# Attention of the next batch interleaved with the inverse transform and projection of this one, with the PSUM banks split 3 and 5

## The chip, the cores and the metric

The kernel runs on one core of one Trainium2 chip. The core has a matrix engine (PE, with its weight loads PEld), a vector engine (DVE), a scalar engine (ACT), a general engine (POOL, which also issues most loads) and a queue engine (SP, which issues the stores). Each engine takes its instructions strictly in the order in which they stand in its queue, and waits on semaphores for the others. The metric is the device time of one execution in microseconds (us). An execution is also profiled: the profile gives the span from the first to the last instruction.

## The reference

Shapes: 8 batches, 8 heads, 576 positions, 64 channels per head; `p` holds 32 packed queries per head. What is computed, cut to what matters:

```python
def sm_attn(qq, kk, vv):                       # softmax attention, scale 1/8
    a = softmax(scale * qq @ kk.T)
    return a @ vv
p_packed = sm_attn(p, k, v)                    # 32 rows per head
x = heads_to_columns(sm_attn(q, p_packed, p_packed))     # [8, 576, 512]
x1, x2, x3 = split(x @ w_proj, 3)              # each [8, 576, 512]
x2_conv = irfft(rfft(x2, axis=1) * rfft(filter, axis=0), n=576, axis=1)
out = (x1 * x2_conv * x3) @ w_out
```

## The kernel before

All loops over batches are unrolled by Python. A scheduler of the framework sets each engine's queue from the order in which the code is written, and may move an instruction ahead when its inputs are due. Tiles come from pools; when a pool has no free buffer, the next writer waits for the last reader of the one that it takes. PSUM has eight banks, and each PSUM tile here takes one.

The work of a batch `b` is written as six stages. `att1`: turn the keys (`kTp`, evicted to `kT` by DVE and ACT in turn), scores of the packed queries (`s1`), their exponentials (`e1`, ACT), the weighted values (`pv`) and sums (`z1`), normalisation (`ppn`, DVE), and the turn of the result (`ppT`) into a buffer `R` (`ppk` in the trace). `att2`: turn the queries (`qTp`, `qTtp`), second scores (`s2`), exponentials (`e2`), sums (`zs`, `zr`, DVE), normalised weights (`a2n`, POOL), and the projection of the packed rows (`qp`, evicted by ACT to `qm`). `att3`: forward transform of the weights (`fp`, `fpt`, evicted by ACT to `fa`) and their turn (`a2tp`, to `a2t`). `moe1`: the spectrum (`f0` to `f4`), its product with the filter's (four DVE products `tt0` to `tt3` from PSUM, two POOL sums, giving `gm`, which has five parts). `moe2`: for eight pieces (four column groups by two halves) two matmuls each for `x1` and `x3`, five for `x2` from `gm` (the inverse transform), an ACT copy `x1s`, and two DVE products `w` and `y`. `moe3`: five output tiles `o` from `y`, scaled by ACT into `os`, stored by SP.

In the loop, iteration `b` writes the attention of `b + 1` first and then the `moe` stages of `b`. All PSUM tiles share one ring of eight banks (`pst`). Before the loop stand the preparation of the filter (`prologue_filter`), the first part of `pack_p` (the packed queries of batch 0), `att1(0)`, the second part of `pack_p` (batches 1 to 7), `att2(0)` and `att3(0)`.

Of the kernel before, what the change touches and what calls it, by code (L numbers as in the profile page):

```python
# [16 lines left out]
P = 128  # L17
# [59 lines left out]
def kernel(  # L77
# [132 lines left out]
    def att1(b):  # L210
        kn, vn, qn, qt = loaded[b]
        e1 = sb.tile([KP, KI, HJ], FP16, tag="e1", name=f"e1_b{b}")
        for g in range(H // 2):
            tp = pst(f"kTp_b{b}", [P, 2, 3, KP], FP16)
            for hh in range(2):
                for ii in range(3):
                    nc.tensor.transpose(tp[:, hh, ii, :], kn[:, 2 * g + hh, ts(ii, P)], ident[0:KP, 0:KP])  # L217
            kT = sb.tile([P, 2, 3, KP], FP16, tag="kT", name=f"kT_b{b}", bufs=4)
            if g % 2 == 0:
                nc.vector.tensor_copy(out=kT[:], in_=tp[:])  # L220
            else:
                nc.scalar.copy(out=kT[:], in_=tp[:])  # L222
            s1 = pst(f"s1_b{b}", [KP, 2, KI, NPK])
            for hh in range(2):
                for ii in range(3):
                    nc.tensor.matmul(s1[:, hh, 2 * ii:2 * ii + 2, :], kT[:, hh, ii, :], pk[:, b, 2 * g + hh, :],  # L226
                                     start=True, stop=True)
            nc.scalar.activation(  # L228
                out=e1[:, :, g * 2 * NPK:(g + 1) * 2 * NPK].rearrange("p i (h j) -> p h i j", h=2),
                in_=s1[:], func=AF.Exp, scale=scale)  # L230
        pv = pst(f"pv_b{b}", [P, 2, 4 * D])
        z1 = pst(f"z1_b{b}", [P, 2])
        for t in range(2):
            for i in range(KI):
                nc.tensor.matmul(pv[:, t, :], e1[:, i, ts(t, P)], vn[:, 4 * t:4 * t + 4, ts(i, D)],  # L235
                                 start=(i == 0), stop=(i == KI - 1))
            for i in range(KI):
                nc.tensor.matmul(z1[:, t:t + 1], e1[:, i, ts(t, P)], ones[0:KP, :],
                                 start=(i == 0), stop=(i == KI - 1))
        rz1 = sb.tile([P, 2], FP32, tag="rz1", name=f"rz1_b{b}")  # L240
        nc.vector.reciprocal(rz1[:], z1[:])
        ppn = sb.tile([P, 2, D], FP16, tag="ppn", name=f"ppn_b{b}")
        for u in range(4):
            r = slice(32 * u, 32 * u + 32)
            nc.vector.tensor_tensor(out=ppn[r, :, :], in0=pv[r, :, ts(u, D)],  # L245
                                    in1=rz1[r, :].unsqueeze(2).broadcast_to([32, 2, D]), op=ALU.mult)
        pT = pst(f"ppT_b{b}", [P, 2, P], FP16)
        for t in range(2):
            for u in range(2):
                nc.tensor.transpose(pT[u * D:(u + 1) * D, t, :], ppn[:, t, :], ident[:])  # L250
        R = rings[b % NR]
# [3 lines left out]
        st[b] = dict(R=R)  # L255

    def att2(b):
        kn, vn, qn, qt = loaded.pop(b)
        s = st[b]
        R = s["R"]  # L260
        Rd = R.rearrange("p (g a) c -> p g (a c)", a=2)
        qT = sb.tile([P, H, 2, P], FP16, tag="qT", name=f"qT_b{b}")
        qTt = sb.tile([P, H // 2, 64], FP16, tag="qTt", name=f"qTt_b{b}")
        for c in range(2):
            tp = pst(f"qTp_b{b}", [P, 4, 2, P], FP16)
            for hh in range(4):
                for ii in range(2):
                    nc.tensor.transpose(tp[:, hh, ii, :], qn[:, 4 * c + hh, ts(ii, P)], ident[:])  # L268
            nc.vector.tensor_copy(out=qT[:, 4 * c:4 * c + 4, :, :], in_=tp[:])
        tp = pst(f"qTtp_b{b}", [P, H // 2, 64], FP16)  # L270
        for g in range(H // 2):
            nc.tensor.transpose(tp[:, g, :], qt[:, 2 * g:2 * g + 2, :], ident[0:64, 0:64])
        nc.vector.tensor_copy(out=qTt[:], in_=tp[:])
# [4 lines left out]
        for ii in range(3):  # L278
# [21 lines left out]
        s["a2n"] = a2n  # L300
        qm = sb.tile([P, 2, DM3], FP16, tag="qm", name=f"qm_b{b}")
        for c in (1, 0, 2):
            for t in range(2):
                qp = pst(f"qp_b{b}", [P, DM])
                for u in range(2):
                    g = 2 * t + u
                    nc.tensor.matmul(qp[u * D:(u + 1) * D, :], Rd[:, g, NPK:3 * NPK], wp[:, g, ts(c, DM)],
                                     start=True, stop=True)
                nc.scalar.copy(out=qm[:, t, ts(c, DM)], in_=qp[:])  # L309
        s["qm"] = qm  # L310

    def att3(b):
        s = st[b]
        a2n = s["a2n"]
        fa = sb.tile([P, 2, 640], FP16, tag="fa", name=f"fa_b{b}")
        for t in range(2):
            fp = pst(f"fp_b{b}", [P, DM])
            for i in range(5):
                n = TILE_SZ[i]
                nc.tensor.matmul(fp[:], a2n[0:n, i, ts(t, P)], wc[0:n, i, 0:DM], start=(i == 0), stop=(i == 4))  # L320
            nc.scalar.copy(out=fa[:, t, 0:DM], in_=fp[:])
        fp = pst(f"fpt_b{b}", [P, 2, 64])
# [7 lines left out]
        a2t = sb.tile([P, 2, S], FP16, tag="a2t", name=f"a2t_b{b}")  # L330
# [6 lines left out]
        s["fa"] = fa  # L337
        s["a2t"] = a2t

    def moe1(b):  # L340
        s = st[b]
        fa, qm = s["fa"], s["qm"]
        gm = sb.tile([P, 5, DM], FP16, tag="gm", name=f"gm_b{b}")
# [7 lines left out]
        for m in range(2):  # L351
            fre = spectrum(m)
            fim = spectrum(2 + m)
            tt = [sb.tile([P, DM], FP32, tag=f"tt{j}", name=f"tt{j}_b{b}", bufs=2) for j in range(4)]
            nc.vector.tensor_tensor(out=tt[0][:], in0=fre[:], in1=hre[:, m, :], op=ALU.mult)
            nc.vector.tensor_tensor(out=tt[1][:], in0=fim[:], in1=him[:, m, :], op=ALU.mult)  # L356
            nc.vector.tensor_tensor(out=tt[2][:], in0=fre[:], in1=him[:, m, :], op=ALU.mult)
            nc.vector.tensor_tensor(out=tt[3][:], in0=fim[:], in1=hre[:, m, :], op=ALU.mult)
            nc.gpsimd.tensor_tensor(out=gm[:, m, :], in0=tt[0][:], in1=tt[1][:], op=ALU.subtract)  # L359
            nc.gpsimd.tensor_tensor(out=gm[:, 2 + m, :], in0=tt[2][:], in1=tt[3][:], op=ALU.add)  # L360
        ft = spectrum(4)
        nc.vector.tensor_tensor(out=gm[:, 4, :], in0=ft[:], in1=htail[:], op=ALU.mult)
        s["gm"] = gm

    def moe2(b):
        s = st[b]
        a2t, qm, gm = s["a2t"], s["qm"], s["gm"]
        y = sb.tile([P, ND, S], FP16, tag="y", name=f"y_b{b}")
        for m in range(ND):
            for e in range(2):  # L370
                cols = ds(e * HALF, HALF)
                x1 = pst(f"x1_b{b}", [P, HALF])
                x3 = pst(f"x3_b{b}", [P, HALF])
                x2 = pst(f"x2_b{b}", [P, HALF])
                for t in range(2):
                    nc.tensor.matmul(x1[:], qm[:, t, ts(m, P)], a2t[:, t, cols], start=(t == 0), stop=(t == 1))  # L376
                for t in range(2):
                    nc.tensor.matmul(x3[:], qm[:, t, ds(2 * DM + m * P, P)], a2t[:, t, cols],  # L378
                                     start=(t == 0), stop=(t == 1))
                for j in range(5):  # L380
                    nc.tensor.matmul(x2[:], gm[:, j, ts(m, P)], ac[:, j, cols], start=(j == 0), stop=(j == 4))  # L381
                x1s = sb.tile([P, HALF], FP32, tag="x1s", name=f"x1s_b{b}", bufs=3)
                nc.scalar.copy(out=x1s[:], in_=x1[:])  # L383
                w = sb.tile([P, HALF], FP32, tag="w", name=f"w_b{b}", bufs=3)
                nc.vector.tensor_tensor(out=w[:], in0=x1s[:], in1=x3[:], op=ALU.mult)  # L385
                nc.vector.scalar_tensor_tensor(out=y[:, m, cols], in0=w[:], scalar=SC_Y, in1=x2[:],  # L386
                                               op0=ALU.mult, op1=ALU.mult)
        s["y"] = y

    def moe3(b):  # L390
        y = st.pop(b)["y"]
        for i in range(5):
            n = TILE_SZ[i]
            o = pst(f"o_b{b}", [P, DM])
            for m in range(ND):
                nc.tensor.matmul(o[0:n, :], y[:, m, COL0[i]:COL0[i] + n], wout[:, m, :], start=(m == 0), stop=(m == ND - 1))  # L396
# [4 lines left out]
            else:  # L401
                tl = out[b, 512:576, :].rearrange("(p e) c -> e p c", e=2)
                nc.sync.dma_start(tl[0], os_[0:32, :])
                nc.sync.dma_start(tl[1], os_[32:64, :])

    pack_p(0, 1, "a")
    prologue_filter()
    att1(0)
    pack_p(1, B, "b")
    att2(0)  # L410
    att3(0)
# [40 lines left out]
```

## Time and profile before

| | |
|---|---|
| median of 3 runs | 357.73 us (356.91 to 357.97) |
| the profiled execution | 357.62 us, its span 355.8 us |
| PE matmul busy, weight loads | 281.9 us (79%), 170.7 us (48%) |
| DVE, ACT, POOL busy | 161.6, 127.1, 94.7 us |
| granted TensorE clock, mean | 0.865 of full speed |
| data read, written | 35.80 MB, 9.44 MB |

Lines with "L" name a line of the kernel's source. Busy time of an engine is the union of its instructions; a matmul's recorded end includes its run-out through the array, so consecutive matmuls overlap in the record, and the distance from one start to the next tells what one costs. A row "x6" is a merged run of six instructions. In square brackets stands how long the engine was idle before a row, and what released it. In rows by stretch, "PEclk" is the share of full clock that the throttle granted.

### The profile page before, as it was taken

How to read it: one execution, taken by the hardware profiler on the slowest of the kernel's cores; microseconds unless marked ns; L12 is line 12 of the kernel's file. 1: busy time of each engine (PE TensorE's matmuls, PEld its weight loads, DVE VectorE, ACT ScalarE, POOL GpSimd, SP SyncE). 2: the span in 40 equal slices, each digit the busy share in tenths (PEclk: the TensorE clock that was granted, in tenths of full speed). 3: DMA queues.
4: the chain of work that ended last, by engine and by line, in shares of the span. 5: the costliest groups of instructions: out<-in, count | busy, mean ns of one | idle time of the engine just before them, and what ended most of it. 6: DMA issues, size and time to landing. Idle time of an engine off the chain costs nothing.

```text
span 355.8 us, 5499 instructions
## 1 busy us (share of the span) xinstructions
PE 281.9 (79%) x2162; PEld 170.7 (48%) x2162; DVE 161.6 (45%) x376; ACT 127.1 (36%) x259; POOL 94.7 (27%) x106
## 2 busy tenths in 40 slices
PE   0596777789868896789777896789778896889995
PEld 0135625536454464546354464546354455546462
DVE  2401721548233851648223851648233941648481
ACT  1324153242516234333516144333516144333333
POOL 7240320344015500433015500433002500133230
PEclk9997675699958998599959998699968997599999
DMA  7999961940369004920378014930300012000303
GB/s 274 216 194 203 201 89 9 144 49 3 133 84 118 0 33 116 157 29 2 133 91 110 1 50 109 143 33 3 133 2 0 0 62 72 2 1 3 134 2 133
DMA packets 35626, 29.08 MB, mean 82 GB/s; under 512 B 7888, under 2 KB 30416, under 8 KB 35600
## 3 DMA queue, kind: packets, MB, share of 16 engines
q0 software_dynamic: 29408, 16.52, 35.2%
q1 hardware_dynamic: 5904, 10.65, 8.7%
q10 hardware_dynamic: 288, 1.56, 1.1%
q8 instruction: 17, 0.28, 0.3%
q14 instruction: 9, 0.07, 0.1%
HBM read 35.80 MB, written 9.44 MB: 127 GB/s over the span
## 4 chain that ended last, share of the span: by engine, by line
PE 61%; DVE 14%; POOL 11%; ACT 6%; issue 3%; DMA 3%; POOLq 0%; DVEq 0%; ACTq 0%
PE x_b L381 11%; PE o_b L396 10%; PE pv_b L235 6%; POOL gm_b L359 6%; PE fp_b L320 5%; PE s_b L226 5%; PE hp L204 4%; PE qTp_b L268 4%; DVE zs_b L291 3%; DMA pnat<-in_p_dram 3%; POOL gm_b L360 3%; PE x_b L378 3%; PE x_b L376 3%; DVE ppn_b L245 3%; ACT kT_b L222 3%
## 5 line engine op out<-in xcount | busy, mean ns | idle before, releaser
L381 PE MATMUL x_b<-ac,gm_b 128*128 128x288 f16 x320 | 51.2, 287 | 6.1 <-POOL gm_b L359 5.0
L383 ACT COPY x1s_b<-x_b 128x288 f32<-128x288 f32 x64 | 25.5, 398 | 80.0 <-PE x_b L376 59.8
L381 PEld LDWEIGHTS <-gm_b 128*128 128x128 f16 x320 | 30.0, 98 | 19.9 <-POOL gm_b L359 10.9
L396 PE MATMUL o_b<-wout,y_b 128*128 128x512 f16 (+1 forms) x160 | 38.2, 381 | 0.3
L295 POOL TENSOR_TENSOR a2n_b<-e_b,zr_b 128x512 f16<-128x512 f16 (+1 forms) x24 | 21.0, 896 | 61.2 <-DVE zr_b L294 61.2
L226 PE MATMUL s_b<-pk,kT_b 128*96 128x64 f16 x192 | 17.1, 232 | 21.9 <-ACT kT_b L222 13.0
L359 POOL TENSOR_TENSOR gm_b<-tt_b,tt_b 128x512 f16<-128x512 f32 x16 | 20.3, 1270 | 50.8 <-DVE tt_b L356 50.8
L220 DVE COPY kT_b<-kTp_b 128x576 f16<-128x576 f16 x16 | 7.3, 458 | 58.0 <-PE kTp_b L217 57.8
L320 PE MATMUL fp_b<-wc,a2n_b 128*128 128x512 f16 (+1 forms) x80 | 24.0, 400 | 11.7 <-ACT qm_b L309 8.5
L290 ACT ACTIVATE e_b<-s_b 128x512 f16<-128x512 f32 (+1 forms) x24 | 10.7, 520 | 60.4 <-PE s_b L284 60.4
L398 ACT ACTIVATE os_b<-o_b 128x512 f32<-128x512 f32 (+1 forms) x40 | 23.8, 596 | 22.1 <-PE o_b L396 22.1
L386 DVE SCALAR_TENSOR_TENSOR y_b<-w_b,x_b 128x288 f16<-128x288 f32 x64 | 26.8, 449 | 7.2 <-PE x_b L381 5.5
L385 DVE TENSOR_TENSOR w_b<-x1s_b,x_b 128x288 f32<-128x288 f32 x64 | 27.4, 448 | 4.5 <-ACT x1s_b L383 3.8
L378 PE MATMUL x_b<-a2t_b,qm_b 128*128 128x288 f16 x128 | 26.1, 286 | 3.9 <-ACT x1s_b L383 3.9
L142 POOL DMA_DIRECT2D kn_b<-in_k_dram x8 | 6.4, 805 | 83.5 <-PE kTp_b L217 81.4
L376 PE MATMUL x_b<-a2t_b,qm_b 128*128 128x288 f16 x128 | 26.1, 286 | 1.0
L336 DVE COPY a2t_b<-a2tp_b 128x576 f16<-128x576 f16 x16 | 7.3, 457 | 42.7 <-PE a2tp_b L335 42.6
L226 PEld LDWEIGHTS <-kT_b 128*96 128x96 f16 x192 | 13.3, 145 | 27.0 <-ACT kT_b L222 15.7
L396 PEld LDWEIGHTS <-y_b 128*128 128x128 f16 (+1 forms) x160 | 14.7, 100 | 21.0 <-DVE y_b L386 4.2
L228 ACT ACTIVATE e_b<-s_b 96x384 f16<-96x384 f32 x32 | 15.6, 486 | 25.5 <-PE s_b L226 25.5
L309 ACT CAST qm_b<-qp_b 128x512 f16<-128x512 f32 x48 | 24.0, 606 | 0.0
L235 PE MATMUL pv_b<-vn_b,e_b 96*128 96x256 f16 x96 | 22.9, 411 | 0.0
(71 smaller groups left out, 428.9 us busy)
## 6 DMA issues: line engine op xcount, KB each, us to landing
out_dram<-os_b SPq DMA_DIRECT2D x32, 256.0 KB, 2.2
kn_b<-in_k_dram POOLq DMA_DIRECT2D x8, 576.0 KB, 6.1
vn_b<-in_v_dram POOLq DMA_DIRECT2D x8, 576.0 KB, 6.3
qn_b<-in_q_dram POOLq DMA_DIRECT2D x8, 512.0 KB, 7.7
wp<-in_moe_w_proj_dram POOLq DMA_DIRECT2D x3, 512.0 KB, 14.8
filt<-in_moe_filter_fft_dram SPq DMA_DIRECT2D x2, 512.0 KB, 8.6
out_dram<-os_b SPq DMA_DIRECT2D x16, 64.0 KB, 1.7
wc<-c_wc ACTq DMA_DIRECT2D x1, 800.0 KB, 4.7
```

The lines of the kernel that those rows point to most:

```text
L226: nc.tensor.matmul(s1[:, hh, 2 * ii:2 * ii + 2, :], kT[:, hh, ii, :], pk[:, b, 2 * g + hh, :], start=True, stop=True)
L235: nc.tensor.matmul(pv[:, t, :], e1[:, i, ts(t, P)], vn[:, 4 * t:4 * t + 4, ts(i, D)], start=(i == 0), stop=(i == KI - 1))
L309: nc.scalar.copy(out=qm[:, t, ts(c, DM)], in_=qp[:])
L320: nc.tensor.matmul(fp[:], a2n[0:n, i, ts(t, P)], wc[0:n, i, 0:DM], start=(i == 0), stop=(i == 4))
L359: nc.gpsimd.tensor_tensor(out=gm[:, m, :], in0=tt[0][:], in1=tt[1][:], op=ALU.subtract)
L376: nc.tensor.matmul(x1[:], qm[:, t, ts(m, P)], a2t[:, t, cols], start=(t == 0), stop=(t == 1))
L378: nc.tensor.matmul(x3[:], qm[:, t, ds(2 * DM + m * P, P)], a2t[:, t, cols], start=(t == 0), stop=(t == 1))
L381: nc.tensor.matmul(x2[:], gm[:, j, ts(m, P)], ac[:, j, cols], start=(j == 0), stop=(j == 4))
L383: nc.scalar.copy(out=x1s[:], in_=x1[:])
L385: nc.vector.tensor_tensor(out=w[:], in0=x1s[:], in1=x3[:], op=ALU.mult)
L386: nc.vector.scalar_tensor_tensor(out=y[:, m, cols], in0=w[:], scalar=SC_Y, in1=x2[:], op0=ALU.mult, op1=ALU.mult)
L396: nc.tensor.matmul(o[0:n, :], y[:, m, COL0[i]:COL0[i] + n], wout[:, m, :], start=(m == 0), stop=(m == ND - 1))
```

## The change

`att1`, `att2`, `att3` and `moe1` become one generator `front(b)`, which stops (`yield`) after each small step with a number for the step's matmul time; `moe2` and `moe3` become `back(b)`. `together` runs two generators and always takes the next step of the one that is less far along (its sum of numbers over 11500 for `front`, over 13200 for `back`). Iteration `b` runs `back(b)` together with `front(b + 1)`, so the spectrum and the filter product of batch `b + 1` are computed an iteration earlier than before. PSUM tiles of `front` have a ring of three banks, those of `back` a ring of five. Inside `front`, the key turns stand ahead of the scores that need them, the query turns move in among the scores, and the products with the filter run `tt0`, `tt2`, `tt1`, `tt3`. The second part of `pack_p` moves into the first iteration.

```diff
-    ps = ctx.enter_context(tc.tile_pool(name="ps", bufs=8, space=bass.MemoryType.PSUM))
+    ps = ctx.enter_context(tc.tile_pool(name="ps", bufs=3, space=bass.MemoryType.PSUM))
+    NA = 3
     def pst(name, shape, dtype=FP32):
-        return ps.tile(shape, dtype, tag="ps", name=name)
+        return ps.tile(shape, dtype, tag="pa", name=name, bufs=NA)
+    def psm(name, shape, dtype=FP32):
+        return ps.tile(shape, dtype, tag="pm", name=name, bufs=8 - NA)
...
+        k_turn(0)
+        yield 260
+        k_turn(1)
+        yield 260
+        score1(0)
+        yield 270
...
+        q_turn(0)
+        yield 450
+        score1(3)
+        yield 270
+        q_turn(1)
+        yield 450
...
         for m in range(2):
             fre = spectrum(m)
-            fim = spectrum(2 + m)
             nc.vector.tensor_tensor(out=tt[0][:], in0=fre[:], in1=hre[:, m, :], op=ALU.mult)
+            nc.vector.tensor_tensor(out=tt[2][:], in0=fre[:], in1=him[:, m, :], op=ALU.mult)
+            yield 430
+            fim = spectrum(2 + m)
             nc.vector.tensor_tensor(out=tt[1][:], in0=fim[:], in1=him[:, m, :], op=ALU.mult)
-            nc.vector.tensor_tensor(out=tt[2][:], in0=fre[:], in1=him[:, m, :], op=ALU.mult)
             nc.vector.tensor_tensor(out=tt[3][:], in0=fim[:], in1=hre[:, m, :], op=ALU.mult)
...
+    def together(*stages):
+        live = [[0.0, total, g] for g, total in stages]
+        while live:
+            x = min(live, key=lambda r: r[0] / r[1])
+            try:
+                x[0] += next(x[2])
+            except StopIteration:
+                live.remove(x)
...
-        if b + 1 < B:
-            att1(b + 1)
-            att2(b + 1)
-            att3(b + 1)
-        moe1(b)
-        moe2(b)
-        moe3(b)
+        if b == 0:
+            pack_p(1, B, "b")
+        stages = [(back(b), BACK)]
+        if b + 1 < B:
+            stages.append((front(b + 1), FRONT))
+        together(*stages)
```

What this makes of the queues is shown at three places. In the names, the number behind `_b` is the batch, and the last number tells tiles of one name apart; rows that repeat, and the weight loads between matmuls, are left out.

PE, key turns and first scores of batch 4, before:

```order
L217 MATMUL kTp_b4_1888<-ident_70,kn_b4_1411 128x96
...
L226 MATMUL s1_b4_1897<-pk_79,kT_b4_1895 96x64
...
L217 MATMUL kTp_b4_1905<-ident_70,kn_b4_1411 128x96
...
L226 MATMUL s1_b4_1914<-pk_79,kT_b4_1912 96x64
...
L217 MATMUL kTp_b4_1922<-ident_70,kn_b4_1411 128x96
```

PE, the same stage for batch 2, now:

```order
L413 MATMUL x1_b1_1098<-a2t_b1_855,qm_b1_760 128x288
...
L230 MATMUL kTp_b2_999<-ident_70,kn_b2_480 128x96
...
L419 MATMUL x3_b1_1103<-a2t_b1_855,qm_b1_760 128x288
...
L426 MATMUL x2_b1_1022<-ac_72,gm_b1_935 128x288
...
L230 MATMUL kTp_b2_1013<-ident_70,kn_b2_480 128x96
...
L426 MATMUL x2_b1_1073<-ac_72,gm_b1_935 128x288
...
L241 MATMUL s1_b2_1029<-pk_79,kT_b2_1006 96x64
```

Each score stood right behind the turn whose eviction it needs; now the next turn and pieces of the inverse transform of batch 1 stand between.

PE, from the spectrum to the first inverse transform, of batch 2, before:

```order
L348 MATMUL f0_b2_1664<-qm_b2_1129,fa_b2_1154 128x512
...
L348 MATMUL f2_b2_1667<-qm_b2_1129,fa_b2_1154 128x512
...
L348 MATMUL f1_b2_1680<-qm_b2_1129,fa_b2_1154 128x512
...
L348 MATMUL f3_b2_1683<-qm_b2_1129,fa_b2_1154 128x512
...
L348 MATMUL f4_b2_1696<-qm_b2_1129,fa_b2_1154 128x512
...
L376 MATMUL x1_b2_1701<-a2t_b2_1181,qm_b2_1129 128x288
...
L378 MATMUL x3_b2_1702<-a2t_b2_1181,qm_b2_1129 128x288
...
L381 MATMUL x2_b2_1703<-ac_72,gm_b2_1663 128x288
```

PE, the same place for batch 1, now:

```order
L384 MATMUL f0_b1_936<-qm_b1_760,fa_b1_854 128x512
...
L384 MATMUL f2_b1_945<-qm_b1_760,fa_b1_854 128x512
...
L434 MATMUL o_b0_952<-wout_74,y_b0_523 64x512
...
L384 MATMUL f1_b1_961<-qm_b1_760,fa_b1_854 128x512
...
L384 MATMUL f3_b1_970<-qm_b1_760,fa_b1_854 128x512
...
L413 MATMUL x1_b1_991<-a2t_b1_855,qm_b1_760 128x288
...
L419 MATMUL x3_b1_1008<-a2t_b1_855,qm_b1_760 128x288
...
L426 MATMUL x2_b1_1022<-ac_72,gm_b1_935 128x288
...
L384 MATMUL f4_b1_977<-qm_b1_760,fa_b1_854 128x512
```

An output tile of batch 0 (`o_b0`) now stands inside the spectrum of batch 1, and the fifth spectrum tile behind the first inverse transform.

DVE, around the key turns, before: two evictions of keys stand alone between the last product of one batch and the normalisation of the next.

```order
L386 SCALAR_TENSOR_TENSOR y_b0_766<-w_b0_900,x2_b0_888 128x288
L220 COPY kT_b2_961<-kTp_b2_954 128x576
L220 COPY kT_b2_995<-kTp_b2_988 128x576
L241 RECIPROCAL rz1_b2_1048<-z1_b2_1023 128x2
L245 TENSOR_TENSOR ppn_b2_1050<-pv_b2_1022,rz1_b2_1048 32x128 x4
```

DVE, the same place, now:

```order
L395 TENSOR_TENSOR tt3_b1_967<-f3_b1_970,hre_75 128x512
L400 TENSOR_TENSOR gm_b1_935<-f4_b1_977,htail_77 128x512
L233 COPY kT_b2_1006<-kTp_b2_999 128x576
L422 TENSOR_TENSOR w_b1_1011<-x1s_b1_994,x3_b1_1008 128x288
L422 TENSOR_TENSOR w_b1_1062<-x1s_b1_1049,x3_b1_1059 128x288
L427 SCALAR_TENSOR_TENSOR y_b1_990<-w_b1_1011,x2_b1_1022 128x288
L233 COPY kT_b2_1044<-kTp_b2_1037 128x576
L427 SCALAR_TENSOR_TENSOR y_b1_990<-w_b1_1062,x2_b1_1073 128x288
```

The first key eviction of batch 2 now follows the filter products of batch 1, and the second follows a product that waits for an inverse transform.

More of the change, by code (lines that the diff above doesn't have):

```diff
@@ L208, with front, k_turn @@
     st = {}
-    def att1(b):
+    def front(b):
         kn, vn, qn, qt = loaded[b]
+        s = st[b] = {}
+        R = rings[b % NR]
+        Rd = R.rearrange("p (g a) c -> p g (a c)", a=2)
         e1 = sb.tile([KP, KI, HJ], FP16, tag="e1", name=f"e1_b{b}")
-        for g in range(H // 2):
+        kTs, qT = {}, sb.tile([P, H, 2, P], FP16, tag="qT", name=f"qT_b{b}")
+        qTt = sb.tile([P, H // 2, 64], FP16, tag="qTt", name=f"qTt_b{b}")
+        def k_turn(g):
             tp = pst(f"kTp_b{b}", [P, 2, 3, KP], FP16)
@@ L254, in att1 @@
                                   in_=pT[u * D:(u + 1) * D].rearrange("p t (h j) -> p (t h) j", j=NPK))
[L255 to L273, printed above, removed]
+        yield 230
         e2 = sb.tile([P, 5, HJ], FP16, tag="e2", name=f"e2_b{b}")
@@ L277, in att2, with score2 @@
         zr = sb.tile([P, 5, H], FP32, tag="zr", name=f"zr_b{b}")
-        for ii in range(3):
+        def score2(ii):
             n = P if ii < 2 else 64
```

107 lines of the change are left out of this document (66 added, 41 removed).

## The prediction

> **What bounds the kernel now.** I read the page's busy times first, then the busy time by stretch, then the waits and the order in time of one iteration (214.8 to 254.8 us; the others look alike).
>
> ```profile
> span 355.8 us, 5499 instructions
> ...
> PE 281.9 (79%) x2162; PEld 170.7 (48%) x2162; DVE 161.6 (45%) x376; ACT 127.1 (36%) x259; POOL 94.7 (27%) x106
> ...
> PEclk9997675699958998599959998699968997599999
> ```
>
> The matrix engine is busy 79% of the span, nothing else half of it, and its clock dips once an iteration. The stretches show that the dip and the idle time belong together:
>
> ```profile
> 28.00:54.20 26.20, 19.33 (x186) 12.55 (x186) 9.50 (x25) 8.87 (x18) 6.20 (x8) 0.69 1.09 157
> ...
> 214.80:254.80 40.00, 32.68 (x260) 20.35 (x260) 19.19 (x46) 14.96 (x32) 11.21 (x12) 0.87 0.44 75
> ...
> 214.80:218.00 3.20, 1.45 (x25) 1.15 (x25) 0.76 (x2) 1.62 (x4) 0.00 (x0) 1.00 0.38 119
> 222.00:226.00 4.00, 2.52 (x26) 2.01 (x25) 1.90 (x8) 0.00 (x0) 0.77 (x1) 0.50 0.90 120
> ...
> 230.00:234.00 4.00, 2.41 (x12) 0.63 (x9) 0.75 (x4) 2.90 (x6) 2.63 (x3) 1.00 1.08 124
> ```
>
> Columns: stretch, its length, busy time of PE, PEld, DVE, ACT, POOL, then granted clock and DMA. One iteration takes 40.0 us. PE works 32.68 us of it, part at half clock; DVE works 19.19 and ACT 14.96, so neither can be the bound before about 20 us. What PE waits for in this iteration (total us, times, longest):
>
> ```profile
> PE s_b L226 <- ACT kT_b L222: 1.7, 2, 0.8
> PE ppT_b L250 <- DVE ppn_b L245: 1.5, 1, 1.5
> ...
> PE fp_b L320 <- ACT qm_b L309: 1.2, 1, 1.2
> ...
> PE s_b L226 <- DVE kT_b L220: 1.1, 2, 0.6
> ...
> PE x_b L381 <- POOL gm_b L359: 0.7, 1, 0.7
> ...
> PE x_b L378 <- ACT x1s_b L383: 0.5, 1, 0.5
> ```
>
> These are 6.7 of the 7.3 us that PE idles, and nearly all are waits inside the attention for an eviction that other work could cover. That is what the change moves in.
>
> **The work that remains: 26.5 us an iteration.** The pieces on PE, as distances from one start to the next:
>
> ```profile
> 217.98 0.45 PE L226 MATMUL s_b<-pk,kT_b 128*96 128x64 f16 x6 [0.55 <-DVE kT_b L220]
> 218.27 0.42 PE L217 MATMUL kTp_b<-ident,kn_b 96*128 96x96 f16 x6
> ...
> 220.04 1.47 PE L235 MATMUL pv_b<-vn_b,e_b 96*128 96x256 f16 x6
> 221.30 0.34 PE L238 MATMUL z_b<-ones,e_b 96*128 96x1 f16 x6
> ...
> 224.93 1.89 PE L268 MATMUL qTp_b<-ident,qn_b 128*128 128x128 f16 x16
> ...
> 227.07 1.14 PE L284 MATMUL s_b<-ppk,qT_b 128*128 128x64 f16 x16
> ...
> 234.60 0.78 PE L326 MATMUL fpt_b<-wc,a2n_b 128*128 128x64 f16 x10
> 235.31 0.99 PE L335 MATMUL a2tp_b<-ident,a2n_b 128*128 128x128 f16 x10
> 236.23 2.33 PE L348 MATMUL f_b<-qm_b,fa_b 128*128 128x512 f16 x10
> 238.40 0.41 PE L376 MATMUL x_b<-a2t_b,qm_b 128*128 128x288 f16 x2
> ...
> 248.31 0.41 PE L376 MATMUL x_b<-a2t_b,qm_b 128*128 128x288 f16 x2
> ...
> 249.41 4.80 PE L396 MATMUL o_b<-wout,y_b 128*128 128x512 f16 x20
> ```
>
> At full clock: a score group 218.27 - 217.98 = 0.29, a key turn 0.42 less a run-out of 0.16 (0.45 - 0.29) = 0.26, four of each 2.2. The stretch from `pv` to the first s2 stands in the half-clock row, so I halve it: `pv` 1.26 to 0.63, with `z` (0.34 less run-out, about 0.2) twice 1.7; query turns and tail 227.07 - 224.93 = 2.14 to 1.1; s2 0.6; `ppT` and the s2 tail about 0.4. `f` is 238.40 - 236.23 = 2.17 for ten, so `fp`, of the same size, 2.3, and `qp`, six such tiles written as two halves side by side, 1.3. `fpt` 0.71, `a2tp` 0.92. Front: 2.2 + 1.7 + 1.1 + 0.6 + 0.4 + 1.3 + 2.3 + 0.7 + 0.9 + 2.2 = 13.4. Back: one piece of the inverse transform is 248.31 to 249.41, 1.10, eight are 8.8; `o`, twenty at `f`'s 0.217, 4.3. Together 26.5 us, with nothing removed: the change only reorders.
>
> **The waits that come: 4.2 us.** I walked the new order by hand from the first spectrum matmul `f0` (time 0), every engine in order, with these durations:
>
> ```profile
> 223.33 1.19 DVE L245 TENSOR_TENSOR ppn_b<-pv_b,rz_b 32x128 f16<-32x128 f32 x4
> ...
> 228.72 1.28 DVE L291 TENSOR_REDUCE zs_b<-e_b 128x16 f32<-128x512 f16 x2 [0.98 <-ACT e_b L290]
> 229.32 3.00 ACT L309 CAST qm_b<-qp_b 128x512 f16<-128x512 f32 x6
> ...
> 230.31 2.63 POOL L295 TENSOR_TENSOR a2n_b<-e_b,zr_b 128x512 f16<-128x512 f16 x3 [1.15 <-DVE zr_b L294]
> ...
> 236.94 0.69 DVE L355 TENSOR_TENSOR tt_b<-f_b,hre 128x512 f32<-128x512 f32 x1
> 237.55 0.68 DVE L356 TENSOR_TENSOR tt_b<-f_b,him 128x512 f32<-128x512 f32 x1
> ...
> 238.38 1.27 POOL L359 TENSOR_TENSOR gm_b<-tt_b,tt_b 128x512 f16<-128x512 f32 x1 [5.44 <-DVE tt_b L356]
> ...
> 240.28 0.40 ACT L383 COPY x1s_b<-x_b 128x288 f32<-128x288 f32 x1 [1.04 <-PE x_b L376]
> ```
>
> - *Filter product.* `f0` is read by DVE 0.71 after its start, a product issues each 0.61; `tt1` is now third, so it ends at 2.6, and POOL (1.27, started 0.15 later) delivers `gm` part 0 at 4.07. PE, with `f0`, `f2`, the last `o`, `f1`, `f3`, `x1`, `x3` (3.1 us), is there at 3.1: wait 1.0. The fourth POOL sum lands at 7.8, PE asks at 7.5: 0.3. The new order of the products costs 0.6 here, the output tile between them hides 0.9.
> - *Copies of x1.* The third `x1` needs the bank of the second, and the third `x3` that of the third `x1`: 0.3 and 0.7, with only a key turn between them.
> - *Keys and scores.* Two turns stand ahead, with pieces of x2 between: evictions 0.46 to 0.64 are met, no wait, where 2.8 us were. The queue cost is on DVE: the third key turn's eviction stands behind a `y` that waits for its x2; it ends at 9.5, and PE asks at 10.0.
> - *Normalisation.* After `z` DVE needs about 1.5 us to the end of `ppn`; a piece (1.1) and the query tail (0.2) cover most: 0.25. The `w` and `y` queued behind `ppn` are late by about 1 us, and five banks let PE run on. The copies to `R` then delay s2 by 0.1.
> - *Projection.* Six `qp` through three banks go at the pace of ACT's evictions, 0.5 each (3.00 for six), against 0.25 of `qp` plus the `x` matmuls between: 0.5 in all, where 1.2 was.
> - *fp.* `a2n` follows 3.7 us after the first s2 and three POOL steps; PE arrives at 22.0 with `a2n` there at 21.7, then waits for the second and third: 0.5. Where POOL is late next, PE stops with x2 and `o` behind it.
> - *y.* `o` needs the last `y`, covered by its first three matmuls: 0.1.
>
> Sum 3.7, and 0.5 for hops that the walk meets with under 0.2 us in hand. One iteration is then 26.5 + 4.2 = 30.7 us, against 40.0. The loads stay ahead of `a2n` on POOL's queue; the last of them wait for the query tail, at 16 us, and `a2n` is due at 20.6, so they fit between; their data are wanted two iterations later. SP stores the same six pieces, now at wider distance.
>
> **Start and end.**
>
> ```profile
> 37.91 1.70 PE L183 MATMUL pT_b<-ident,pnat 128*64 128x128 f16 x28
> ...
> 39.01 2.53 DVE L185 COPY pk<-pT_b 64x1024 f16<-64x1024 f16 x4 [0.26 <-PE pT_b L183]
> ...
> 53.34 0.66 PE L217 MATMUL kTp_b<-ident,kn_b 96*128 96x96 f16 x6
> ...
> 334.09 2.33 PE L348 MATMUL f_b<-qm_b,fa_b 128*128 128x512 f16 x10
> ```
>
> The first front runs alone; `f0` would have stood at 53.3. Moving the packing out (its copies hold the query evictions up to 41.5) and the query turns into the score waits saves 4 to 8 us; I take 6.3: `f0` at 47.0. The first iteration carries the packing, between 0.9 (its PE time at full clock) and 4.6 (1.6 PE, then 2.5 DVE, plus hops) more: 3.0. From the last `f0` to the end takes 355.8 - 334.1 = 21.7 now, and 22.0 with the changed product order. Seven distances between first spectra: 7 x 30.7 + 3.0 = 217.9. Span 47.0 + 217.9 + 22.0 = 286.9; the profiled execution is 357.62 for a span of 355.8, so 1.8 on top: 288.7, about **289 us**. That execution stands 0.1 below the median of the runs.
>
> **Rivals.**
>
> *The clock still falls: 318 us.* The clock fell after the stretch in which PE was busy 1.45 of 3.20 us (45%), and stayed full through one with 2.41 of 4.00 (60%). The loosest stretch of my walk, 3.1 to 6.8 us after `f0`, is near 50%: in between. The dip now is about 10.2 us long at 0.50 (by the clock column); the same would cost 5.1 us an iteration, less about 1.0 of waits that it swallows: 34.8 us, 7 x 4.1 more, 318; with a dip of a third of it, near 300. [...]
>
> *All but the filter product is covered: 269 us.* With 1.3 us of waits left an iteration is 27.8, 7 x 2.9 less. For it: DVE has 19 us of work in 28; against: its queue is strict, and it serves both streams.
>
> *Three banks serialise: slower, 394 us.* A front has 32 PSUM tiles. Were each late by its eviction (0.6 as for `qm`), 32 x 0.6 = 19.2 would come on top of 26.5: 45.7 an iteration, 7 x 15 more. It decides above (40.0 - 26.5) / 32 = 0.42 us a tile. Against: on most places a step of `back`, 0.25 to 0.9 us, stands between two front tiles. A part of it (0.2 a tile) gives 32.9 us, 304.
>
> That the scheduler undoes the interleaving is excluded by the order shown.
>
> **Chances.** My forecast, 280 to 298: 0.60. Clock, 298 to 325: 0.20. Tight, 267 to 280: 0.12. Partial serialisation, 300 to 340: 0.05. Serial, slower: 0.02. No change: 0.01; about 0.3% is what a measurement here can tell. The range 274 to 308 leaves out half of the tight and half of the clock case, and most of the last three. Faster 0.97, same 0.01, slower 0.02.
>
> **What would show it.** PE busy per iteration near 27 to 28 us in a period near 30.7, granted clock 1.00 throughout the loop; the longest PE wait the one for `gm`, about 1 us, then `x1s`; no wait of scores for `kT`; POOL's wait for `tt` products shorter. I am wrong if the clock column dips, if `qp` or `fp` waits exceed 1.5 us an iteration, or if `w` and `y`, queued behind attention work on DVE, hold the five banks.

## The result and the profile after

The changed kernel takes 282.88 us (282.46 to 284.24) where the kernel before takes 357.85 (356.91 to 358.15): a ratio of 0.7915, 95% interval 0.7884 to 0.7946. The forecast was 289, with a range of 274 to 308. The profiled execution took 282.67 us, its span is 280.9. Where the executions of a kernel below fall into a faster and a slower group, the ratio is that of the faster group; for `b_keys` the range of all is given instead. The page after, its busy times and the clock:

```profile
span 280.9 us, 5474 instructions
...
PE 249.9 (89%) x2162; PEld 144.3 (51%) x2162; DVE 162.4 (58%) x376; ACT 128.9 (46%) x259; POOL 94.8 (34%) x106
...
PEclk9999979999999999999999999999999999999999
```

PE has the same 2162 instructions as before, but 32 us less busy time, and the dips of the clock inside the loop are gone, in which matmuls take longer (the sixteen of the second scores 1.14 us from 227.07 at a clock of 0.50 before, 0.63 from 93.09 at 1.00 now); the one digit that is left belongs to the first front, which runs alone. By stretch, with the columns of the prediction: the first iteration, the second, and all six full ones together.

```profile
44.11:75.57 31.46, 29.63 (x286) 17.90 (x285) 22.21 (x51) 13.92 (x29) 11.22 (x12) 1.00 0.72 111
75.57:105.91 30.34, 29.04 (x261) 17.27 (x260) 19.15 (x45) 15.27 (x31) 11.22 (x12) 1.00 0.57 99
75.57:257.94 182.37, 174.24 (x1562) 103.58 (x1561) 115.02 (x270) 91.64 (x186) 60.03 (x62) 1.00 0.41 79
```

The borders are the starts of the first spectrum matmul `f0`. An iteration took 40.0 us and takes 182.37 / 6 = 30.4; PE is idle (182.37 - 174.24) / 6 = 1.36 us of it, where it was 7.3, at a full clock (1.00), where it was 0.87. The longest waits of PE over the whole span, apart from 11.9 us for the load of `p` ahead of the loop (total us, times, longest):

```profile
PE x_b L426 <- POOL gm_b L396: 5.4, 8, 1.4
PE x_b L419 <- ACT x1s_b L415: 3.4, 7, 0.5
PE x_b L426 <- POOL gm_b L397: 1.7, 8, 0.4
PE ppT_b L304 <- DVE ppn_b L296: 1.5, 1, 1.5
```

No wait of the scores for `kT`, of `fp` for `qm` or of `ppT` for `ppn` is left in the loop (the one for `ppn` is in the first front). What is left in the loop stands in one place, in the 8 us behind the start of the spectrum. PE, DVE and POOL there, in order of time:

```profile
75.57 1.03 PE L384 MATMUL f_b<-qm_b,fa_b 128*128 128x512 f16 x4
...
76.53 1.05 PE L434 MATMUL o_b<-wout,y_b 128*64 128x512 f16 x4
76.88 0.68 DVE L391 TENSOR_TENSOR tt_b<-f_b,him 128x512 f32<-128x512 f32 x1
77.48 0.68 DVE L394 TENSOR_TENSOR tt_b<-f_b,him 128x512 f32<-128x512 f32 x1
...
78.24 1.27 POOL L396 TENSOR_TENSOR gm_b<-tt_b,tt_b 128x512 f16<-128x512 f32 x1 [10.21 <-DVE tt_b L394]
...
79.56 0.30 PE L426 MATMUL x_b<-ac,gm_b 128*128 128x288 f16 x1 [0.53 <-POOL gm_b L396]
...
82.18 0.41 PE L419 MATMUL x_b<-a2t_b,qm_b 128*128 128x288 f16 x2 [0.49 <-ACT x1s_b L415]
```

POOL's first sum needs the product that DVE now makes third; it starts 2.67 us after `f0`, and PE stands idle for the end of it.

### The profile page after: what moved, and what is told of

The parts are those of the page before. It is cut to its first block, busy times and chain, and to the rows that moved or that the text cites. A ratio compares the mean times of both kernels' runs of the same rounds, so it can differ in the third digit from the quotient of the medians.

```text
span 280.9 us, 5474 instructions
## 1 busy us (share of the span) xinstructions
PE 249.9 (89%) x2162; PEld 144.3 (51%) x2162; DVE 162.4 (58%) x376; ACT 128.9 (46%) x259; POOL 94.8 (34%) x106
## 4 chain that ended last, share of the span: by engine, by line
PE 66%; POOL 12%; DMA 10%; DVE 7%; issue 2%; ACT 1%; POOLq 0%; DVEq 0%; ACTq 0%
PE x_b L426 14%; PE o_b L434 11%; PE fp_b L360 7%; POOL gm_b L397 6%; PE qp_b L343 6%; POOL gm_b L396 6%; DMA vn_b<-in_v_dram 5%; DMA kn_b<-in_k_dram 5%; PE x_b L413 5%; PE x_b L419 4%; PE pv_b L284 4%; PE s_b L241 3%; PE a2tp_b L376 3%; PE qTp_b L251 2%; DVE tt_b L390 2%
## 5 line engine op out<-in xcount | busy, mean ns | idle before, releaser
L426 PE MATMUL x_b<-ac,gm_b 128*128 128x288 f16 x320 | 59.4, 287 | 7.1 <-POOL gm_b L396 5.4
L396 POOL TENSOR_TENSOR gm_b<-tt_b,tt_b 128x512 f16<-128x512 f32 x16 | 20.3, 1270 | 76.4 <-DVE tt_b L394 76.4
L434 PE MATMUL o_b<-wout,y_b 128*128 128x512 f16 (+1 forms) x160 | 40.4, 382 | 0.0
L427 DVE SCALAR_TENSOR_TENSOR y_b<-w_b,x_b 128x288 f16<-128x288 f32 x64 | 28.7, 451 | 19.8 <-PE x_b L426 17.9
L437 ACT ACTIVATE os_b<-o_b 128x512 f32<-128x512 f32 (+1 forms) x40 | 23.8, 596 | 33.7 <-PE o_b L434 33.7
L419 PE MATMUL x_b<-a2t_b,qm_b 128*128 128x288 f16 x128 | 28.6, 287 | 3.4 <-ACT x1s_b L415 3.4
L413 PE MATMUL x_b<-a2t_b,qm_b 128*128 128x288 f16 x128 | 28.6, 287 | 1.0
L345 ACT CAST qm_b<-qp_b 128x512 f16<-128x512 f32 x48 | 26.4, 596 | 0.8
L360 PE MATMUL fp_b<-wc,a2n_b 128*128 128x512 f16 (+1 forms) x80 | 22.2, 389 | 0.0
L384 PE MATMUL f_b<-qm_b,fa_b 128*128 128x512 f16 x80 | 21.3, 380 | 0.0
L397 POOL TENSOR_TENSOR gm_b<-tt_b,tt_b 128x512 f16<-128x512 f32 x16 | 20.3, 1272 | 0.0
L343 PE MATMUL qp_b<-wp,ppk 128*64 128x512 f16 x96 | 18.5, 418 | 0.3 <-ACT e_b L326 0.2
L419 PEld LDWEIGHTS <-qm_b 128*128 128x128 f16 x128 | 11.9, 97 | 10.0 <-issue 7.9
L413 PEld LDWEIGHTS <-qm_b 128*128 128x128 f16 x128 | 11.1, 97 | 8.8 <-issue 3.2
```

## The experiments

The time left open which part did it. The change has four parts: the written interleaving (I), the split of the PSUM banks (R), the filter product an iteration earlier (S), and the new order inside the attention (K). Two smaller ones, the packing that moves into the first iteration and the order of the filter products, stay as they are in each kernel unless it is said; the packing was not tested by itself. The theory at the start was that I is the cause and R its condition; the rival, that the clock or the order K is. Each row of a table below is one kernel; ratios are to the kernel before, on the same chip.

**Parts taken from the changed kernel.** `seq8` undoes I and R, `seq35` undoes I alone, `inter8` undoes R alone.

```diff
 seq35, seq8:
-        stages = [(back(b), BACK)]
         if b + 1 < B:
-            stages.append((front(b + 1), FRONT))
-        together(*stages)
+            for _ in front(b + 1):
+                pass
+        for _ in back(b):
+            pass
 seq8, inter8 (pst and psm): one ring for all tiles
-    ... bufs=3 ... tag="pa", bufs=NA ... tag="pm", bufs=8 - NA
+    ... bufs=8 ... tag="ps"
```

`seq8`:

> The changed kernel with its fronts and backs one after the other again (front of batch b+1 whole, then back of b) and all PSUM tiles in one ring of eight; the order inside a front, and the filter product in the front, stay. Theory A (the steps of back cover the waits of front): those waits are open again, PE alone has 13.4 us of work in a front that takes 18 to 22, the clock dips as before, an iteration is 35 us or more and the time above 315 us. Theory B (the gain is the new order inside the front and the filter product an iteration early, the interleaving adds little): a front is 13.4 + 1.5 (normalisation) + 0.7 (copies to R) + 1.6 (a2n) + 0.3 = 17.5, a back 13.1 + 0.5, together 31.1 at full clock, 7 x 0.8 more than the changed kernel: about 289 us, granted clock above 0.97.

`seq35`:

> As the kernel in sequence with one ring of eight, but with the split of 3 and 5 banks kept. Theory A: above 320 us. Theory B: the projection goes at the pace of ACT's evictions through three banks, 1.2 to 1.5 us an iteration more than with eight: about 298 us. Either way slower than with one ring of eight.

`inter8`:

> The changed kernel, interleaved, with one ring of eight banks in place of 3 and 5. If the split matters (a shared ring lets one stream take the banks of the other), more than 290 us. If not, within 1% of the changed kernel, 280 to 286 us: the walk of its order met few waits for banks.

| kernel | parts | us | ratio (95%) |
|---|---|---|---|
| changed | I R S K | 282.88 | 0.7915 (0.7884 to 0.7946) |
| `seq8` | S K | 311.99 | 0.8747 (0.8674 to 0.8820) |
| `seq35` | R S K | 279.90 | 0.7824 (0.7777 to 0.7871) |
| `inter8` | I S K | 303.30 | 0.8473 (0.8406 to 0.8541) |

This overturned the theory. Without the written interleaving the kernel is not slower but 1% faster; without the split, with the interleaving written out, it loses 20 us. `seq35` is not sequential on PE: pieces of `x` of one batch stand among spectrum tiles and key turns of the next, placed there by the scheduler.

```profile
102.58 0.59 PE L384 MATMUL f_b<-qm_b,fa_b 128*128 128x512 f16 x2
103.02 0.78 PE L426 MATMUL x_b<-ac,gm_b 128*128 128x288 f16 x5
103.63 0.41 PE L413 MATMUL x_b<-a2t_b,qm_b 128*128 128x288 f16 x2
103.87 0.42 PE L230 MATMUL kTp_b<-ident,kn_b 96*128 96x96 f16 x6
```

In `inter8` they are interleaved as written, but the tiles take their banks from one ring in turn, and PE waits longer at the known place. That the ring costs the 20 us is shown, since nothing else differs; that the turn of the banks leaves PE no other work there is read from the order. Its waits behind the spectrum:

```profile
121.78 0.42 PE L426 MATMUL x_b<-ac,gm_b 128*128 128x288 f16 x2 [1.98 <-POOL gm_b L396]
123.01 0.42 PE L426 MATMUL x_b<-ac,gm_b 128*128 128x288 f16 x2 [0.80 <-POOL gm_b L397]
```

`seq8` is sequential on PE, and there the waits inside the attention stay:

```profile
166.18 0.42 PE L304 MATMUL ppT_b<-ident,ppn_b 128*64 128x128 f16 x4 [1.48 <-DVE ppn_b L296]
167.30 1.03 PE L320 MATMUL s_b<-ppk,qT_b 128*128 128x64 f16 x16 [0.69 <-DVE ppk L306]
```

**The clock by itself.** `b_warm` is the kernel before with two or three extra matmuls ahead of each of the last three scores, into a bank of their own, results unused (the ring then has seven banks).

```diff
+    def fill(n, kT):
+        for _ in range(n):
+            nc.tensor.matmul(junk[0:KP, :], kT[:, 0, 0, :], wc[:, 0, 0:DM], start=True, stop=True)
...
+            if g:
+                fill(2 + g % 2, last)
+            last = kT
```

> The kernel before with eight matmuls that nobody reads put between the key turns and the first scores of each batch (128x512, about 0.22 us each at full clock, in waits of 0.55 to 0.85 us), with one PSUM bank for them; nothing else changes. Theory C (most of the gain is the clock): PE is then busy above 60% in that stretch, the clock stays full, each iteration loses the 10.2 us at half clock, some 4.5 us: 357.8 - 7 x 4.5 = 326 us, granted clock above 0.97. If waits and not the clock hold the iteration: 350 us or more at a full clock. If the filling does not keep the clock, 357 to 362 and the clock near 0.87.

Measured 347.99 to 352.43 us, 0.9777 (0.9725 to 0.9829), with a mean clock of 0.935 to 0.945 over the span, where the kernel before had 0.855 to 0.879. So none of the three expectations was met in full. The execution that was profiled took 356.36 us, with a mean clock of 0.927. One iteration of it:

```profile
200.00:240.00 40.00, 34.18 (x268) 20.14 (x268) 19.61 (x45) 14.83 (x31) 11.21 (x12) 0.91 0.43 75
```

In this iteration the clock is 0.91, against 0.87. With the scores filled it held through them (1.00 from 204 to 224), and was near half (0.53 in the second row) 2.6 us behind the next long wait, which is the one for `ppn`:

```profile
221.88 0.30 PE L260 MATMUL ppT_b<-ident,ppn_b 128*64 128x128 f16 x4 [1.49 <-DVE ppn_b L255]
```

```profile
224.50:227.70 3.20, 3.18 (x22) 1.78 (x19) 2.03 (x6) 3.01 (x7) 1.83 (x3) 0.53 1.35 195
```

A clock kept up for part of the iteration gave 8 us. That isn't its worth by itself: PE's waits for `gm` grew from 5.0 to 12.5 us over the span, probably because the ring has seven banks, which was not tested apart, and the eight matmuls take time of their own. What the clock alone is worth stays open.

**Parts added to the kernel before.** `b_spectrum` adds S, `b_keys` adds the order of key and query turns of K, `b_split` adds R, `b_split_spec` adds R and S.

```diff
 b_spectrum, b_split_spec:
     att3(0)
+    moe1(0)
...
             att3(b + 1)
-        moe1(b)
+            moe1(b + 1)
         moe2(b)
 b_split, b_split_spec: x1, x3, x2 and o
-                x1 = pst(f"x1_b{b}", [P, HALF])
+                x1 = psm(f"x1_b{b}", [P, HALF])
...
 b_keys (the calls joined on two lines):
+        k_turn(0); k_turn(1); score1(0); k_turn(2); score1(1); k_turn(3); score1(2)
+        q_turn(0); score1(3); q_turn(1)
```

`b_spectrum`:

> The kernel before with one edit: the filter product (moe1) of batch b+1 is written right after the attention of b+1, an iteration earlier, ahead of the inverse transform of b. One ring of eight banks, old order inside the attention; in PE's queue the two batches still stand one after the other. Theory A (the early spectrum removes only what the product itself makes PE wait for): the wait for gm and its neighbourhood, 0.7 to 2 us an iteration, so 342 to 353. Theory B (it is what brought the sequential version with new order to 312, through the clock): 312 to 325. If 357, the early spectrum by itself is worth nothing.

`b_keys`:

> The kernel before with one edit: the key turns stand one ahead of the scores that need them, and the two query turns stand among the last scores, as in the changed kernel. Nothing else. Theory A (the new order inside the attention is the larger part of the 46 us that the sequential version gained): the four waits for kT, 2.8 us an iteration, go, and with them the stretch of 45% busy time ahead of the clock's fall, so part of the 5 us that the half-clock costs: 320 to 338. Theory B (only the waits go, the clock falls at the next wait, for ppn): 358 less 8 times 2.8, 335 to 345, with the clock as low as before.

`b_split`:

> The kernel before with one edit: the PSUM banks split 3 (attention and spectrum) and 5 (x1, x3, x2, o). In PE's queue the pieces of x of batch b still stand behind the attention of b+1, since its spectrum is written behind that attention. Theory A (the split gives nothing by itself; it gives the scheduler freedom only where the data are early enough): 354 to 362, perhaps slower by the ring of three at qp. Theory B (the split by itself is what interleaves and is worth the 20 to 30 us that it was worth in the new order): 325 to 340.

`b_split_spec`:

> The kernel before with two edits: the filter product of batch b+1 written right after the attention of b+1 (before the inverse transform of b), and the PSUM banks split 3 and 5. No interleaving in the code, old order inside the attention. In PE's queue pieces of x of batch b now stand among the attention of b+1, from the second key turn on. Theory A (early spectrum and split together are what lets the two batches overlap, and that is most of the gain): 280 to 295, clock 0.97 or more, period 30 to 32. Theory B (the order inside the attention is an independent 20 to 40 us, which the overlap does not cover): 300 to 320. The order inside the attention is then the difference to the 279.9 us of the version that has all three but no interleaving in the code.

| kernel | parts | us | ratio (95%) |
|---|---|---|---|
| `b_spectrum` | S | 347.44 | 0.9719 (0.9663 to 0.9775) |
| `b_split` | R | 351.23 | 0.9830 (0.9790 to 0.9871) |
| `b_split_spec` | R S | 289.26 | 0.8092 (0.8062 to 0.8122) |
| `b_keys` | K (turns) | 320.14 | between 312.99 and 321.44 |

(357.57 before on that chip.) Theory A held for `b_spectrum` and `b_split_spec`. The median of `b_keys` lies at its lower edge, with two of the four executions below it. For `b_split` A was nearer than B, but the split alone gave 6 us where A had nothing. One iteration of each, in the order of the table (for `b_keys` from the execution of 312.99 us):

```profile
120.05:158.56 38.51, 31.92 (x261) 20.61 (x261) 18.73 (x46) 14.95 (x31) 11.22 (x12) 0.87 0.47 77
```

```profile
113.68:152.85 39.17, 32.95 (x261) 20.00 (x261) 19.43 (x46) 14.86 (x31) 11.24 (x12) 0.87 0.45 76
```

```profile
107.26:137.66 30.40, 28.81 (x259) 16.89 (x258) 18.95 (x46) 14.52 (x31) 11.22 (x12) 1.00 0.56 98
```

```profile
130.72:165.49 34.77, 30.31 (x262) 18.85 (x261) 19.19 (x46) 14.94 (x31) 11.21 (x12) 0.95 0.49 86
```

S saves 10 us, R 6, both together 68: each is the condition of the other. The order in the queues gives a reason. With S alone `gm`, which `x2` needs, is ready early, but the tiles of `x` take banks from the ring behind all tiles of the next attention, and PE's queue stays sequential. With R alone they have their own banks, but the spectrum that `x2` needs is written behind that attention. With both, the scheduler moves them into the waits. PE in `b_split_spec`, where the stage of keys and scores is in its old order:

```profile
118.67 0.42 PE L220 MATMUL kTp_b<-ident,kn_b 96*128 96x96 f16 x6
118.93 0.41 PE L379 MATMUL x_b<-a2t_b,qm_b 128*128 128x288 f16 x2
119.18 0.41 PE L381 MATMUL x_b<-a2t_b,qm_b 128*128 128x288 f16 x2
119.43 0.41 PE L384 MATMUL x_b<-ac,gm_b 128*128 128x288 f16 x2
119.94 0.46 PE L229 MATMUL s_b<-pk,kT_b 128*96 128x64 f16 x6
```

Between a key turn and its score stand six matmuls of the batch before, in a kernel whose code has no interleaving at all. K is a second way to part of the same gain: it takes away most of the waits for `kT` directly (21.8 us over the span before, 2.4 in `b_keys`) and is worth 37 us by the median, but what it takes is mostly what the overlap would have covered. On top of R and S, K together with the moved packing and the new order of the products is worth 289.26 - 279.90 = 9 us, most of it ahead of the loop: `f0` of the first batch starts at 52.37 in `b_split_spec` and at 45.50 in `seq35`. How much of that is K and how much the packing was not separated.

**The rest of the waits.** `tt_old` is the changed kernel with the filter products in the old order; `seq26` and `seq44` are `seq35` with the banks split 2 and 6, and 4 and 4.

```diff
 tt_old:
             nc.vector.tensor_tensor(out=tt[0][:], in0=fre[:], in1=hre[:, m, :], op=ALU.mult)
-            nc.vector.tensor_tensor(out=tt[2][:], in0=fre[:], in1=him[:, m, :], op=ALU.mult)
...
             nc.vector.tensor_tensor(out=tt[1][:], in0=fim[:], in1=him[:, m, :], op=ALU.mult)
+            nc.vector.tensor_tensor(out=tt[2][:], in0=fre[:], in1=him[:, m, :], op=ALU.mult)
 seq26, seq44:
-    NA = 3
+    NA = 2   (seq44: 4)
```

`tt_old`:

> The changed kernel with the four products of the filter in the old order (tt0, tt1, tt2, tt3, all behind both spectrum tiles) and nothing else undone. In the changed kernel PE waits 0.53 us for the first gm sum and 0.2 for a later one in each iteration. Theory A (the new product order makes that wait, by the 0.6 us that one product takes on DVE): the waits for gm go, period 30.34 to about 29.8, tail 0.5 shorter: 278 to 280.5. Theory B (PE has then only the next wait of the chain x1, w, x2, or the second spectrum tile waits for its bank): 281.5 to 285.

`seq26`:

> The version written in sequence with split rings (279.9 us) with the banks split 2 and 6 instead of 3 and 5. Theory A (three banks in front are more than needed, since x pieces stand between front tiles, and the waits left are for banks of the five: x2 for w 0.54 us an iteration): period 29.7 to about 29.2, 275 to 279. Theory B (with two banks the tiles of the front that follow one another without x between them, scores, query turns, qp, f, wait for their evictions; 32 tiles an iteration of which a third would pay 0.2 to 0.4 us): period 32 to 34, 295 to 312.

`seq44`:

> The version written in sequence with split rings (279.9 us) with the banks split 4 and 4. Theory A (the three banks of the front are not what PE waits for; with four for the back, x1 and x3 wait sooner for w and y): 281 to 287. Theory B (the ring of three holds the front's tiles back, at qp and at f above all, and the fourth bank frees the scheduler to mix them more evenly): 275 to 279.

| kernel | us | ratio (95%) |
|---|---|---|
| `tt_old` | 278.77 | 0.7825 (0.7796 to 0.7854) |
| `seq26` | 282.38 | 0.7918 (0.7893 to 0.7942) |
| `seq44` | 291.68 | 0.8140 (0.8090 to 0.8189) |

`tt_old` came out as theory A said, but not as it reasoned. The wait for the first sum did go, yet the third sum is now late by as much; what else went is the wait for `x1s`, 3.4 us in the changed kernel and 0.5 here, and most of that for the second and fourth sums.

```profile
PE x_b L426 <- POOL gm_b L396: 5.6, 8, 1.4
...
PE x_b L419 <- ACT x1s_b L415: 0.5, 1, 0.5
PE x_b L426 <- POOL gm_b L397: 0.3, 1, 0.3
```

`seq44` went the way of theory A, beyond its range, and is slower than `seq35` by 11 to 12 us. Its longest wait in the loop is new:

```profile
PE x_b L413 <- DVE w_b L422: 10.4, 7, 1.8
```

Four banks for the back are too few: an `x1` waits for the bank that `w` still reads. `seq26` met neither theory. Six full iterations of `seq35` and of `seq26`:

```profile
71.83:247.84 176.01, 170.81 (x1542) 103.08 (x1541) 111.35 (x267) 86.29 (x183) 59.99 (x62) 1.00 0.43 82
```

```profile
81.11:255.27 174.16, 172.49 (x1551) 102.19 (x1550) 114.89 (x270) 85.14 (x185) 60.01 (x62) 1.00 0.43 81
```

In the loop two banks for the front are not slower than three (29.0 us an iteration against 29.3). The loss lies ahead of it, where the first front has no `x` pieces between its tiles: its `f0` starts at 50.38, against 45.50, part of it at a low clock: 0.65 from 26.00 to 40.00, where `seq35` has 0.84.

```profile
26.00:40.00 14.00, 10.41 (x115) 8.00 (x114) 4.49 (x12) 3.72 (x8) 3.59 (x5) 0.65 1.35 201
```

**A version that beats both.** `best` is `tt_old` with one more number changed.

```diff
-    FRONT, BACK = 11500.0, 13200.0
+    FRONT, BACK = 14500.0, 13200.0
```

> The changed kernel with two edits: the products in the old order (278.8 us alone), and the number for the front in the interleaving 14500 instead of 11500, so that the front steps are taken sooner: the front then ends before the last output tiles of the back, four of which and two key turns stand between f0 and the first x2. Theory A (the gm wait, 0.6 us an iteration still, is only a matter of how much work stands between f0 and the first x2; PE is then at x2 some 6.7 us after f0, the first sum is there 3.4 and the third 5.9 us after it): the wait goes, period 29.56 to about 28.9, 273 to 276. Theory B (the front drawn closer together then waits itself, for a2n at fp and for the banks of qp): 278 to 284.

Measured 272.16 us (271.7 to 272.5), 0.7640 (0.7613 to 0.7668): by the two ratios 3.5% under the changed kernel, and faster than theory A forecast (273 to 276). Six full iterations:

```profile
74.93:246.02 171.09, 170.94 (x1561) 103.40 (x1560) 116.20 (x270) 87.91 (x187) 60.03 (x62) 1.00 0.44 84
```

28.52 us an iteration, and PE idle for 0.15 us in six of them. By this trace the loop is at the work of the matrix engine in this order; less time there would need fewer or cheaper matmuls.

## Why the prediction was right, and where it was not

The total held, and the changes that it forecast came: a full clock in the loop and no waits inside the attention. That the iteration came out within 0.3 us is luck, since its two parts were off by about 2 us each, in opposite directions. In the order of its terms:

- **`f0` of the first batch: 47.0 forecast, 44.11 measured.** The saving in the first front was taken as 6.3 out of 4 to 8 us; it was 53.3 - 44.1 = 9.2, outside these bounds. The term counted waits and packing only, but the clock rose too: 0.90 from 26.80 to 44.11, where 28.00 to 54.20 before had 0.69. The two were not separated.
- **First iteration: 33.7, measured 31.46.** The packing was priced at 3.0; against the mean iteration of 30.4 it cost 1.1, near the lower bound of 0.9. The bound "its PE time" was the nearer one: PE waits there for `gm` only, and for none of DVE's copies of the packing.
- **Iteration: 30.7, measured 30.4.** The work was put at 26.5. `best`, which leaves PE no wait, shows 28.46 in one iteration (from 74.93 to 103.39). Summed by distances from start to start there: `qp` 1.92 against 1.3, `fp` 2.55 against 2.3, the eight `x` pieces 9.83 against 8.8, `o` 4.53 against 4.3; the other pieces came out as forecast or slightly under. The waits were put at 4.2; taking that work for both orders, 30.4 - 28.5 = 1.9 remained, of which 1.36 stand in the trace as idle PE.
- **End, from the last `f0`: 22.0, measured 280.9 - 257.94 = 22.96.** An output tile of the batch before, 0.99 us, stands inside the last spectrum and was not counted.

Together -2.9 - 2.2 - 1.8 + 1.0 = -5.9, but for rounding the 6.0 us between 286.9 and 280.9.

The step that failed in the work is the price of a matmul, taken from one run of `f` or of `x` and used everywhere. It failed in two ways.

- `fp` ("of the same size" as `f`) and `o` ("twenty at `f`'s 0.217") cost more even in one run: ten `fp` in `seq35` take 97.70 - 95.14 = 2.56, and twenty `o` in `seq8` 158.94 - 154.41 = 4.53. That is what they cost in `best`, so the interleaving adds nothing to them. The row of `o` in the prediction, 4.80 with its run-out, already said more than 4.3.
- `qp` and `x` cost more because they stand in turn, and this is where "the change only reorders" failed. In the changed kernel, `qp` pairs and `x2` pairs with their weight loads:

```profile
63.90 0.11 PEld L343 LDWEIGHTS <-ppk 128*64 128x64 f16 x2 [0.24 <-issue]
63.90 0.41 PE L343 MATMUL qp_b<-wp,ppk 128*64 128x512 f16 x2
64.23 0.11 PEld L426 LDWEIGHTS <-gm_b 128*128 128x128 f16 x2 [0.23 <-issue]
64.24 0.42 PE L426 MATMUL x_b<-ac,gm_b 128*128 128x288 f16 x2
64.59 0.41 PE L343 MATMUL qp_b<-wp,ppk 128*64 128x512 f16 x2
```

A pair of each takes 0.34 to 0.35 us from start to start. For `qp` the forecast had 0.22, and two `x2` matmuls had been 0.245. Not every turn costs that: `x1` and `x3` pairs in turn stay at 0.25. The weight loads (PEld) show a difference: here each starts together with its matmul, while between `x1` and `x3` the load starts ahead (78.51 for the matmul at 78.63). In these rows it is the change between weights of 64 and of 128 columns that the load doesn't run ahead of. That this is the cause fits the rows but was not tested by a run.

Of the waits, the walk named the places and their order rightly: `gm` first (1.0 and 0.3 forecast; 0.53 and 0.17 in the iteration from 75.57), then `x1s` (1.0; 0.49). The 0.6 us of the product order came out in size in `tt_old`, (182.37 - 177.75) / 6 = 0.77 an iteration, its six taking 177.75; but the total wait for the first and third sums stayed (5.4 and 5.6 us), and what went are the waits for `x1s` and for the second and fourth sums.

```profile
76.40:254.15 177.75, 173.44 (x1562) 103.15 (x1561) 115.64 (x270) 91.54 (x186) 60.05 (x62) 1.00 0.42 81
```

What didn't come are the waits at `ppn`, `qp`, `a2n` and `y`, 1.35 together, and the allowance of 0.5. Two of the signs that were named did not come either: PE is busy 174.24 / 6 = 29.0 us an iteration, not 27 to 28, and POOL's wait for the `tt` products got longer, not shorter (76.4 us over the span, 50.8 before).

The rivals. The clock did not fall in the loop (1.00). The loosest stretch was forecast near 50% busy; from the second iteration on, the loosest two microseconds behind the spectrum are at 67%. In the first iteration they are at 32% (second row), and the clock held there too, at 1.00 in both rows.

```profile
81.60:83.60 2.00, 1.34 (x14) 0.90 (x13) 1.23 (x4) 1.00 (x2) 1.60 (x2) 1.00 0.00 0
46.20:48.20 2.00, 0.64 (x4) 0.13 (x3) 2.00 (x4) 0.06 (x1) 1.48 (x2) 1.00 1.56 196
```

Three banks did not serialise, and two did not either: with `x` pieces between its tiles the front needs few (29.0 us an iteration in `seq26` with two, 29.3 in `seq35` with three). The risk was on the other side, in the back's ring, which the prediction named last ("`w` and `y` ... hold the five banks"); with four it cost 11 to 12 us. The clock stayed at 1.00 in the loop with rings of three and of two. The rival of 269 us came true only with `best`, which covers the filter product as well, and at 272, since the rival rested on the same low sum of work.

What the prediction did not see is the cause. It credited the written interleaving. The runs show that the split of the banks and the early filter product suffice for 68 of the 75 us, that the scheduler then interleaves by itself, and that the written order was, as it stood, 3 us slower than none.

An account of one iteration, from the rows shown, by length, clock lost (length times one minus the clock) and idle PE: before 40.0, 5.2, 7.3; `b_keys` 34.8, 1.7, 4.5; changed 30.4, 0, 1.4; `best` 28.5, 0, 0. Both losses go together: in the rows shown the clock fell behind stretches in which PE waits (before, to 0.50 behind one with PE busy 1.45 of 3.20 us; in `b_keys`, to 0.52 behind one with 0.07 of 1.50). So the gain cannot be divided into a part for the waits and a part for the clock.

## What to carry to other kernels

Before writing an interleaving by hand, look at what keeps the scheduler from making one: a ring of buffers shared by two streams hands them out in the order of the code, and one input written too late holds back a whole stream. Take both away together, since each alone gave under 3% here and the two 19%. If that can't be had, the order inside one stream is worth a try by itself (`b_keys`, 37 us by the median). In the sum for an interleaved order, price each kind of matmul from its own rows, and where it will alternate from places where it already does, and ask of each wait how much other work stands in the queue ahead of it: one number that moved output tiles into the last gap was worth 2.4%.

## What was not expected of the hardware

The clock's fall after a wait is not a function of the wait alone. In `b_keys` PE waits 1.49 us for `ppn` ahead of 190.43 and again ahead of 225.61. Once the clock fell right behind that wait, to 0.52 (first two rows), once it held at 1.00 behind the same wait (last two) and fell no sooner than at a further one, of 1.64 us for `qm` (0.85 from 228.60 to 240.00).

```profile
189.00:190.50 1.50, 0.07 (x2) 0.07 (x4) 1.30 (x5) 0.00 (x0) 0.85 (x2) 1.00 1.30 201
190.50:194.00 3.50, 3.13 (x36) 2.44 (x38) 2.11 (x6) 1.87 (x5) 1.14 (x2) 0.52 1.41 196
223.60:225.10 1.50, 0.53 (x10) 0.40 (x8) 0.87 (x4) 0.00 (x0) 0.00 (x0) 1.00 0.00 0
225.10:228.60 3.50, 2.52 (x40) 1.81 (x40) 2.18 (x7) 1.49 (x4) 0.00 (x0) 1.00 0.02 5
```

The executions of `b_keys` differ by 8 us (312.99 to 321.44), with a mean clock of 0.954 in the shortest and 0.935 in the longest. What decides when the clock falls stays open; no kernel here was made to measure it.
